# Four token tiles' finishing steps moved from the first half of a loop to the stretch behind it

## The chip, the cores and the metric

One core of one Trainium2 chip runs the whole kernel. The metric is the device time of one execution in microseconds (us), the median over several runs. All tensors between engines live in the core's on-chip memory; matmul results go to PSUM, an accumulation memory from which ScalarE (ACT) or VectorE (DVE) must copy them before the space can be used again. TensorE (PE) multiplies, DVE and ACT do element-wise work, SyncE (SP) issues nearly all DMAs, GpSimd (POOL) does small things. Each engine runs its own instructions in the order in which they were written out; only semaphores join the engines.

## The reference

The input x is 2048 tokens by 1024 channels. The output mixes two branches with a gate for each token:

```python
g = sigmoid((x * gate_w).sum(-1, keepdims=True))
# branch a: 2-D real FFT over (tokens, channels), product with W, back
X = rfft2(x, axes=(-2, -1)) * (w_r + 1j * w_i)
a = irfft2(X, s=(S, D))
# branch b: a diagonal complex recurrence over the tokens
Lam_bar = exp(dt * Lam);  B_bar = ((Lam_bar - 1) / Lam)[:, None] * Bmat
Bu = einsum("bld,pd->blp", x, B_bar)
for t in range(L):
    h = Lam_bar * h + Bu[:, t, :]
y = 2 * einsum("blp,dp->bld", hseq, Cmat).real + x * Dskip
return g * a + (1 - g) * y
```

x and all weights are bf16, and so is the output.

## The kernel before

The FFT branch (generator `gfnet`) is done as dense transforms with small matrices. Its steps are mixed with the first recurrence units and are over at about 200 us; what stays of it is the tile `ZT`, the spectrum after all transforms but the last one along the channels.

The recurrence branch is cut into 8 chunks of 256 tokens and two halves q of the 1024 states, 16 **units** in all. `unit(c, q)` makes 64 matmuls (L209) into two PSUM tiles `psu`, one for the real and one for the imaginary part; ACT copies each into the tile `h` (L211); DVE then rotates, scans (L223) and rotates back (L215 to L234), with a small carry to the next chunk (L227 to L229). A unit of a later chunk must follow the unit of the chunk before.

A chunk holds two **token tiles** of 128 tokens, 16 tiles in all, numbered tb. For each there are two steps:

- `c_gemm(tb)`, the **C product**: 32 matmuls of `h` with `CT` (L462) and 8 of `xT` with a diagonal (L466), into the PSUM tile `ps_y`.
- `finish(tb, psy)`: 8 matmuls (L483) do the last inverse transform of the tile from `ZT` into the PSUM tile `ps_id`; ACT scales it by the gate into a part of the tile `raw` (L486); DVE unfolds it in four operations (L488, L489, L491, L492) into the tile `ga`; DVE adds the C product (L500); SP stores `ga` to the output (L501).

The first four token tiles are **early** (`NEARLY = 4`). Their C products are made while the FFT branch still runs; `early(tb)` stores them as f32 halves in a scratch in DRAM (L475). When `finish` runs for such a tile, it has no `psy`: SP loads each half back into the tile `yl` (L497) and DVE adds it (L498), half by half.

Four buffer rules matter around the change:

- `ps_id` and both `psu` of a unit come from one pool with two PSUM buffers (`psU`). A third use waits until ACT has emptied the first.
- `ps_y` has its own pool of two (`psA`), emptied by DVE's L500.
- The part of `raw` that ACT writes at L486 is chosen by `tb % 2`. Two tiles in a row with the same parity share it: ACT may write the second one only when DVE has read the first (L488, L489).
- `yl` has one buffer, so the second half's load waits for the first half's add, and the next tile's first load for this tile's second add.

The main loop goes over the last 8 units. In it `todo` is the list of tiles 4 to 15, and `late` that of tiles 0 to 3. After the loop four tiles of `todo` are left, 12 to 15. We call the loop's eight passes iterations 0 to 7, and what follows the **tail**. No planner sets the order here: each engine's order is essentially that of the code, with small steps that the framework moves across each other by its priorities.

Of the kernel before, what the change touches and what calls it, by code (L numbers as in the profile page):

```python
# [84 lines left out]
def kernel(  # L85
# [370 lines left out]
    def c_gemm(tb, pool=None, tag="ps"):  # L456
        c, tq = tb // 2, tb % 2
        psy = (pool or psA).tile([P, D], FP32, name="ps_y", tag=tag)
        for dh in range(2):
            for i in range(16):  # L460
                jb, ri = i // 2, i % 2
                nc.tensor.matmul(psy[:, 512 * dh:512 * (dh + 1)], lhsT=hs[c, jb // 4][:, ri, jb % 4, P * tq:P * (tq + 1)],  # L462
                                 rhs=CT[ri][:, jb, 512 * dh:512 * (dh + 1)], start=(i == 0), stop=False)
            for d4 in range(4):
                d8 = 4 * dh + d4
                nc.tensor.matmul(psy[:, P * d8:P * (d8 + 1)], lhsT=xT[:, d8, P * tb:P * (tb + 1)],  # L466
                                 rhs=fft["dgD"][:, d8, :], start=False, stop=(d4 == 3))
        return psy
# [8 lines left out]
    def finish(tb, psy=None):  # L477
        ZT_t = fft["ZT"]
        pse = psU.tile([P, 4, H], FP32, name="ps_id", tag="psu")
        for slot, (cls, ri) in enumerate(((0, 0), (1, 1), (0, 1), (1, 0))):  # L480
            for kb in range(2):
                i = 4 * cls + 2 * kb + ri
                nc.tensor.matmul(pse[:, slot, :], lhsT=ZT_t[:, i, tb, :], rhs=fft["Gi"][:, i, :],  # L483
                                 start=(kb == 0), stop=(kb == 1))
        part = raw[:, D * (2 + tb % 2):D * (3 + tb % 2)].rearrange("p (s c n) -> p s c n", s=2, c=2)
        nc.scalar.activation(out=part.rearrange("p s c n -> p (s c) n"), in_=pse, func=ACT.Copy, scale=gB[:, tb:tb + 1])  # L486
        eo = raw[:, D * (4 + tb % 2):D * (5 + tb % 2)].rearrange("p (c k) -> p c k", c=2)
        nc.vector.tensor_add(out=eo[:, :, 0:H], in0=part[:, 0], in1=part[:, 1])  # L488
        nc.vector.tensor_sub(out=eo[:, :, K - 1:H - 1:-1], in0=part[:, 0], in1=part[:, 1])  # L489
        ga = fft["gq"].tile([P, 2, K], BF16, name="ga")  # L490
        nc.vector.tensor_add(out=ga[:, 0], in0=eo[:, 0], in1=eo[:, 1])  # L491
        nc.vector.tensor_sub(out=ga[:, 1], in0=eo[:, 0], in1=eo[:, 1])  # L492
        o = ga.rearrange("p h n -> p (h n)")
        if psy is None:
            for hf in range(2):
                ye = fft["gq"].tile([P, K], FP32, name="yl", bufs=1)
                nc.sync.dma_start(out=ye, in_=y_dram[tb, hf])  # L497
                nc.vector.tensor_add(out=ga[:, hf], in0=ye, in1=ga[:, hf])  # L498
        else:
            nc.vector.scalar_tensor_tensor(out=o, in0=psy, scalar=omg[:, tb:tb + 1], in1=o, op0=ALU.mult, op1=ALU.add)  # L500
        nc.sync.dma_start(out=out2[P * tb:P * (tb + 1), :], in_=o)  # L501
# [160 lines left out]
    late = list(range(NEARLY))  # L662
    for c in range(4, 8):
        for q in range(2):
            unit(c, q)
            tb = todo.pop(0)
            finish(tb, c_gemm(tb))
            if late:
                finish(late.pop(0))
    for tb in todo:  # L670
        finish(tb, c_gemm(tb))


# [28 lines left out]
```

## Time and profile before

| what | us |
|---|---|
| median of 3 runs (lowest to highest) | 413.42 (412.79 to 415.82) |
| the profiled execution, its own time | 413.43 |
| its span, first to last instruction | 411.6 |
| PE busy | 365.1 (89%) |
| DVE busy | 307.8 (75%) |
| ACT busy | 168.9 (41%) |
| POOL busy | 28.8 (7%) |

The profiled execution takes 1.83 us more than its span, and its time is that of the median. The loop's first matmul starts at 225.49 us of the span, the tail's first at 370.42, and the last output DMA is issued at 408.58. In a row of the timeline stand the start, the duration, the engine, the line, the operation with its output and inputs, the shapes and a count; in square brackets follows how long the engine sat idle before it, and what ended that wait. The word issue there means that the profile shows nothing that was waited for. In a row of the waits stand who waited, for what, and the total, the count and the longest, in us. A view of windows cuts the span into stretches and gives the busy time of each engine with the count of instructions, the granted clock of TensorE (1.00 is full), the DMA share and GB/s.

### The profile page before, as it was taken

What the parts mean: (1) busy time and instruction counts of PE and PEld (TensorE: products, weight loads), DVE (VectorE), ACT (ScalarE), POOL (GpSimd) and SP (SyncE); (2) the same over time, 40 slices, a digit from 0 to 9 for tenths busy, and PEclk for the clock granted to TensorE, in tenths of its full rate; (3) what the DMA queues carried; (4) which work ended last, traced back from release to release, by engine and by line L of the source; (5) the groups of instructions that cost most, each with busy time, mean ns of one, the idle gap of its engine ahead of it and who ended that gap; (6) DMA issues with size and microseconds to landing.
All of it is one profiled execution on the core that took longest, in us unless ns stands there. A gap on an engine that the chain in (4) does not pass through costs nothing. (4 is left out here: it accounts for less than half of the span.)

```text
span 411.6 us, 6481 instructions
## 1 busy us (share of the span) xinstructions
PE 365.1 (89%) x2601; PEld 239.7 (58%) x2601; DVE 307.8 (75%) x477; ACT 168.9 (41%) x210; POOL 28.8 (7%) x68
## 2 busy tenths in 40 slices
PE   4868998999797998999999988689796999999992
PEld 4836555667574454457766765556464767764551
DVE  2873598196989898990098897959696999999332
ACT  2759797664221588848721212121212113202111
POOL 7600011162000000000000000000000000000000
PEclk9879999999899699999999999969898999999997
DMA  7999921987742288659310103011111000000001
GB/s 207 340 201 208 212 77 53 223 191 148 179 146 79 82 274 314 225 173 292 123 53 2 51 2 100 3 51 51 53 51 53 25 27 2 25 27 16 36 32 45
DMA packets 58077, 45.84 MB, mean 111 GB/s; under 512 B 38720, under 2 KB 43200, under 8 KB 57792
## 3 DMA queue, kind: packets, MB, share of 16 engines
q1 hardware_dynamic: 57616, 45.41, 38.8%
q0 software_dynamic: 352, 0.02, 0.7%
q8 instruction: 20, 0.33, 0.3%
q14 instruction: 9, 0.07, 0.1%
q10 hardware_dynamic: 80, 0.01, 0.0%
HBM read 22.35 MB, written 14.69 MB: 90 GB/s over the span
## 5 line engine op out<-in xcount | busy, mean ns | idle before, releaser
L209 PE MATMUL psu<-xT,BT 128*128 128x256 bf16 x1024 | 129.3, 283 | 14.8 <-ACT raw L486 13.4
L209 PEld LDWEIGHTS <-BT 128*128 128x128 bf16 x1024 | 103.1, 101 | 38.8 <-issue 15.8
L462 PE MATMUL ps_y<-CT,h 128*128 128x512 bf16 x512 | 117.2, 379 | 0.7 <-DVE ga L500 0.7
L462 PEld LDWEIGHTS <-h 128*128 128x128 bf16 x512 | 49.5, 98 | 53.2 <-issue 0.9
L223 DVE TENSOR_TENSOR_SCAN h<-rz,h 128x1024 bf16<-128x1024 f32 x32 | 71.8, 2278 | 0.3
L486 ACT ACTIVATE raw<-ps_id,gB 128x1024 bf16<-128x1024 f32 x16 | 17.8, 1113 | 109.1 <-PE ps_id L483 85.5
L215 DVE TENSOR_TENSOR su<-h,tab 128x2048 bf16<-128x2048 bf16 x16 | 19.6, 1222 | 48.6 <-ACT h L211 48.5
L211 ACT CAST h<-psu 128x1024 bf16<-128x1024 f32 x32 | 32.3, 1010 | 57.1 <-PE psu L209 57.1
L249 PE MATMUL ps_fd<-G_sb,preT 128*128 128x512 bf16 x128 | 32.0, 397 | 4.7 <-ACT X L252 4.3
L249 PEld LDWEIGHTS <-preT 128*128 128x128 bf16 x128 | 18.6, 146 | 15.2 <-issue 8.5
L252 ACT CAST X<-ps_fd 128x1024 bf16<-128x1024 f32 x16 | 20.7, 1304 | 9.3 <-PE ps_fd L249 9.3
L359 ACT CAST X<-ps_s 128x1024 bf16<-128x1024 f32 x16 | 16.2, 1013 | 17.1 <-PE ps_s L357 17.1
L216 DVE TENSOR_TENSOR h<-h,tab 128x2048 bf16<-128x2048 bf16 x16 | 19.6, 1222 | 0.5
L488 DVE TENSOR_TENSOR raw<-raw 128x512 bf16<-128x512 bf16 x16 | 6.7, 418 | 17.3 <-ACT raw L486 17.3
L232 DVE TENSOR_TENSOR h<-h,tab 128x2048 bf16<-128x2048 bf16 x16 | 19.6, 1222 | 0.1
L231 DVE TENSOR_TENSOR sg<-h,tab 128x2048 bf16<-128x2048 bf16 x16 | 19.5, 1217 | 0.1
L507 PE MATMUL pt<-ident,BT 128*128 128x128 bf16 x128 | 12.8, 271 | 5.6 <-DMA BT<-in_A_x_dram 5.5
L380 ACT CAST C<-ps_is 128x1024 bf16<-128x1024 f32 x16 | 16.2, 1014 | 3.6 <-PE ps_is L378 3.2
L396 ACT CAST ZT<-ps_is 128x1024 bf16<-128x1024 f32 x16 | 16.1, 1012 | 3.0 <-PE ps_is L394 2.3
L392 PE MATMUL ps_is<-R_sb,raw 128*128 128x256 bf16 x64 | 14.8, 272 | 1.7 <-DMA raw<-turn_scratch 1.7
L500 DVE SCALAR_TENSOR_TENSOR ga<-ps_y,omg,ga 128x1024 bf16<-128x1024 f32 x12 | 15.4, 1283 | 1.2
L483 PE MATMUL ps_id<-raw,ZT 128*128 128x256 bf16 x128 | 15.9, 273 | 0.0
(188 smaller groups left out, 445.9 us busy)
## 6 DMA issues: line engine op xcount, KB each, us to landing
BT<-in_A_x_dram SPq DMA_DIRECT2D x8, 512.0 KB, 6.4
turn_scratch<-A SPq DMA_DIRECT2D x16, 256.0 KB, 2.9
Bb<-turn_scratch SPq DMA_DIRECT2D x16, 256.0 KB, 3.9
turn_scratch<-C SPq DMA_DIRECT2D x16, 256.0 KB, 3.1
raw<-turn_scratch SPq DMA_DIRECT2D x16, 256.0 KB, 5.3
out_dram<-ga SPq DMA_DIRECT2D x16, 256.0 KB, 2.0
W_b<-in_A_w_r_dram SPq DMA_DIRECT2D x16, 128.0 KB, 4.2
W_b<-in_A_w_i_dram SPq DMA_DIRECT2D x16, 128.0 KB, 3.8
```

What stands on the lines that cost most here:

```text
L209: nc.tensor.matmul(psu[:, j, :], lhsT=BT[4 * q + j][:, ri, d8, :], rhs=xT[:, d8, TC * c:TC * (c + 1)], start=(d8 == 0), stop=(d8 == 7))
L211: nc.scalar.copy(out=u[:, ri], in_=psu)
L215: nc.vector.tensor_mul(out=su, in0=u[:, ::-1], in1=bc(1))
L216: nc.vector.tensor_mul(out=u, in0=u, in1=bc(0))
L223: nc.vector.tensor_tensor_scan(out=seg, data0=rz[:, js].rearrange("p j t -> p (j t)"), data1=seg, initial=0.0, op0=ALU.mult, op1=ALU.add)
L231: nc.vector.tensor_mul(out=sg, in0=u[:, ::-1], in1=bc(3))
L232: nc.vector.tensor_mul(out=u, in0=u, in1=bc(2))
L249: nc.tensor.matmul(ps[:, cls, :], lhsT=preT_A[:, cls, d4, j, :], rhs=G_sb[:, cls, d4, :], start=(d4 == 0), stop=(d4 == 3))
L252: nc.scalar.copy(out=X1.rearrange("p r (i c) -> p c r i", c=2), in_=ps.rearrange("p c (r i) -> p c r i", r=2))
L359: nc.scalar.copy(out=X2, in_=ps2)
L462: nc.tensor.matmul(psy[:, 512 * dh:512 * (dh + 1)], lhsT=hs[c, jb // 4][:, ri, jb % 4, P * tq:P * (tq + 1)], rhs=CT[ri][:, jb, 512 * dh:51 ...
L486: nc.scalar.activation(out=part.rearrange("p s c n -> p (s c) n"), in_=pse, func=ACT.Copy, scale=gB[:, tb:tb + 1])
```

## The change

In the loop, `finish` is no longer called for a late tile. In the tail, each C product's `finish` is followed by that of one late tile, so the tail's order is 12, 0, 13, 1, 14, 2, 15, 3. All else is left: the same operations, the same buffers, the same tiles.

```diff
             unit(c, q)
             tb = todo.pop(0)
             finish(tb, c_gemm(tb))
-            if late:
-                finish(late.pop(0))
     for tb in todo:
         finish(tb, c_gemm(tb))
+        finish(late.pop(0))
```

What moves on ACT, in the loop's iterations 0 to 2. `psu` is a unit's PSUM tile, `ps_id` that of a finish. Before:

```order
L486 ACTIVATE raw<-ps_id,gB 128x1024 x2
L211 CAST h<-psu 128x1024 x2
L486 ACTIVATE raw<-ps_id,gB 128x1024 x2
L211 CAST h<-psu 128x1024 x2
L486 ACTIVATE raw<-ps_id,gB 128x1024 x2
```

And the same place now:

```order
L486 ACTIVATE raw<-ps_id,gB 128x1024
L211 CAST h<-psu 128x1024 x2
L486 ACTIVATE raw<-ps_id,gB 128x1024
L211 CAST h<-psu 128x1024 x2
L486 ACTIVATE raw<-ps_id,gB 128x1024
```

The second scaling between two units' copies is gone from iterations 0 to 3, and the row at ACT's end counts 9 in place of 5.

What moves on SP, in the tail. The numbers tell the buffers' uses apart: before, `ga_3911` is tile 11 and `ga_3969` to `ga_4143` are tiles 12 to 15.

```order
L501 DMA out_0_dram<-ga_3911 128x1024
L501 DMA out_0_dram<-ga_3969 128x1024
L501 DMA out_0_dram<-ga_4027 128x1024
L501 DMA out_0_dram<-ga_4085 128x1024
L501 DMA out_0_dram<-ga_4143 128x1024
```

Now `ga_3881`, `ga_3961` and `ga_4041` are tiles 12, 13 and 14, `ga_3898` and `ga_3978` are tiles 0 and 1:

```order
L501 DMA out_0_dram<-ga_3881 128x1024
L497 DMA yl_3904<-y_scratch_60 128x512
L501 DMA out_0_dram<-ga_3898 128x1024
L497 DMA yl_3981<-y_scratch_60 128x512
L501 DMA out_0_dram<-ga_3961 128x1024
L497 DMA yl_3984<-y_scratch_60 128x512
L501 DMA out_0_dram<-ga_3978 128x1024
L497 DMA yl_4061<-y_scratch_60 128x512
L501 DMA out_0_dram<-ga_4041 128x1024
```

Seven of the eight loads of `yl` now stand between the tail's stores; the eighth (tile 0's first half) stands far ahead in both kernels.

What ends DVE's work. Before, tile 15 (`ga_4143`) is the last:

```order
L488 TENSOR_TENSOR raw_512<-raw_512 128x2x256
L489 TENSOR_TENSOR raw_512<-raw_512 128x2x256
L491 TENSOR_TENSOR ga_4143<-raw_512 128x512
L492 TENSOR_TENSOR ga_4143<-raw_512 128x512
L500 SCALAR_TENSOR_TENSOR ga_4143<-ps_y_4090,omg_809,ga_4143 128x1024
```

Now tile 15 is `ga_4121`, and tile 3 (`ga_4138`) is the last:

```order
L500 SCALAR_TENSOR_TENSOR ga_4121<-ps_y_4068,omg_809,ga_4121 128x1024
L488 TENSOR_TENSOR raw_512<-raw_512 128x2x256
L489 TENSOR_TENSOR raw_512<-raw_512 128x2x256
L491 TENSOR_TENSOR ga_4138<-raw_512 128x512
L492 TENSOR_TENSOR ga_4138<-raw_512 128x512
L498 TENSOR_TENSOR ga_4138<-yl_4141,ga_4138 128x512
L498 TENSOR_TENSOR ga_4138<-yl_4144,ga_4138 128x512
```

Behind tile 15's L500 there are now six more DVE operations ahead of the last store, with a load of `yl` between the last two.

## The prediction

> **What bounds the kernel now.** I read the page first, for the engine that works most and the wait that ends its idle time.
>
> ```profile
> span 411.6 us, 6481 instructions
> ...
> L209 PE MATMUL psu<-xT,BT 128*128 128x256 bf16 x1024 | 129.3, 283 | 14.8 <-ACT raw L486 13.4
> ```
>
> The units' matmuls stood idle 14.8 us, 13.4 of them until a scaling of a finish (L486) was over. All of that must lie where finishes run, so I cut the loop and the tail into windows at the starts of the PE work: five rows for iterations 0 to 4, three for 5 to 7, one for the tail.
>
> ```profile
> 225.49:242.07 16.58, 16.58 (x125) 11.60 (x123) 14.58 (x16) 4.40 (x5) 0.00 (x0) 1.00 0.09 33
> 242.07:260.82 18.75, 16.31 (x122) 11.38 (x121) 15.62 (x26) 4.14 (x4) 0.00 (x0) 1.00 0.17 57
> 260.82:284.00 23.18, 18.76 (x122) 12.53 (x121) 18.64 (x27) 4.14 (x4) 0.00 (x0) 0.85 0.14 46
> 284.00:305.25 21.25, 17.97 (x121) 12.28 (x120) 17.51 (x26) 4.14 (x4) 0.00 (x0) 0.92 0.16 50
> 305.25:324.78 19.53, 16.25 (x111) 11.02 (x110) 16.13 (x25) 3.03 (x3) 0.00 (x0) 0.91 0.12 42
> 324.78:340.00 15.22, 15.22 (x115) 10.62 (x113) 14.91 (x20) 3.14 (x3) 0.00 (x0) 1.00 0.05 18
> 340.00:355.21 15.21, 15.21 (x114) 10.62 (x112) 14.90 (x20) 3.14 (x3) 0.00 (x0) 1.00 0.05 18
> 355.21:370.42 15.21, 15.21 (x114) 10.61 (x112) 14.83 (x17) 3.14 (x3) 0.00 (x0) 1.00 0.05 18
> 370.42:404.39 33.97, 33.23 (x194) 17.36 (x191) 17.23 (x26) 4.46 (x4) 0.00 (x0) 1.00 0.08 31
> ```
>
> Here are two regimes of one loop. Iterations 5 to 7, which have one finish each, take 15.21 us with PE busy in all of it and DVE in 14.9. Iterations 0 to 3 have a second, late finish, and with what they leave behind in iteration 4 the five windows take 99.29 us, or 19.9 each. In the tail PE is full again, and DVE is busy in half of it.
>
> The waits from 222 us on say how the late finish does that (waiter, what it waited for, total, count, longest):
>
> ```profile
> ACT raw L486 <- DVE raw L489: 23.6, 4, 7.0
> ...
> PE psu L209 <- ACT raw L486: 13.4, 4, 4.4
> DVE su L215 <- ACT h L211: 12.5, 4, 4.2
> ```
>
> Each has a count of 4, the number of late finishes. The timeline of all engines at iteration 2's end and iteration 3's start shows the links in order:
>
> ```profile
> 280.63 4.48 DVE L223 TENSOR_TENSOR_SCAN h<-rz,h 128x1024 bf16<-128x1024 f32 x2
> ...
> 281.76 1.91 PE L483 MATMUL ps_id<-raw,ZT 128*128 128x256 bf16 x16
> 282.83 1.11 ACT L486 ACTIVATE raw<-ps_id,gB 128x1024 bf16<-128x1024 f32 x1 [6.78 <-PE ps_id L483]
> ...
> 284.00 3.65 PE L209 MATMUL psu<-xT,BT 128*128 128x256 bf16 x32
> ...
> 289.24 0.42 DVE L489 TENSOR_TENSOR raw<-raw 128x512 bf16<-128x512 bf16 x1
> ...
> 289.77 1.11 ACT L486 ACTIVATE raw<-ps_id,gB 128x1024 bf16<-128x1024 f32 x1 [5.82 <-DVE raw L489]
> ...
> 290.93 5.32 PE L209 MATMUL psu<-xT,BT 128*128 128x256 bf16 x32 [3.28 <-ACT raw L486]
> ```
>
> PE makes both finishes' matmuls at once (16 at 281.76). ACT scales the first at 282.83. The second is of a tile with the same parity (6 and 2), so ACT must wait until DVE has read the first; but DVE is in the unit's scans and gets to L489 only at 289.24. Until 290.88 the late `ps_id` holds one of the two `psU` buffers, so PE can make one half of the next unit (284.00) and then stands for 3.28 us. That delays ACT's copies and DVE's next unit (the 12.5 us of the third wait). It is a circle through three engines that only the late finish closes.
>
> **The change, part by part.** The loop first. Its other rows:
>
> ```profile
> 225.49 7.15 PE L209 MATMUL psu<-xT,BT 128*128 128x256 bf16 x64
> ...
> 248.17 3.65 PE L209 MATMUL psu<-xT,BT 128*128 128x256 bf16 x32 [2.44 <-ACT raw L486]
> ...
> 268.89 6.11 PE L209 MATMUL psu<-xT,BT 128*128 128x256 bf16 x32 [4.42 <-ACT raw L486]
> ...
> 312.18 4.97 PE L209 MATMUL psu<-xT,BT 128*128 128x256 bf16 x32 [3.28 <-ACT raw L486]
> ...
> 323.91 1.04 PE L483 MATMUL ps_id<-raw,ZT 128*128 128x256 bf16 x8
> ```
>
> Without the late finishes, iterations 0 to 4 have on each engine the order that 5 to 7 have, so I take their 15.21. The loop's PE work then lasts from 225.49 to 225.49 + 8 x 15.21 = 347.17, where before it ended at 370.42: **23.25 us less**. The parts confirm it. Gone are four times eight L483 matmuls (1.91 - 1.04 = 0.87 each, 3.5 in all); the waits of 2.44, 4.42, 3.28 and 3.28 (13.4); and the slow matmuls behind three of these waits: 32 of them took 6.11, 5.32 and 4.97 where 3.65 is normal (5.4). Together 22.3; the 0.9 left is small gaps. DVE, at 14.8 to 14.9 busy of 15.21, becomes the next limit; it is the cover that has nearly nothing left, and I put 0.7 as the upper bound of what it adds over eight iterations (the 0.72 that PE waits for DVE at the loop's end, row 379.53 below); below zero is excluded, since PE has no idle time to give.
>
> Of the slow matmuls, the trace has full speed behind 2.44 us of idleness, and a lowered clock behind 3.28 and more (0.85 to 0.92 in these windows). [...] The measured rows decide: I count all three as gone.
>
> The tail next. Its PE rows, and the last steps:
>
> ```profile
> 379.53 3.61 PE L462 MATMUL ps_y<-CT,h 128*128 128x512 bf16 x16 [0.72 <-DVE ga L500]
> ...
> 387.76 3.62 PE L462 MATMUL ps_y<-CT,h 128*128 128x512 bf16 x16
> ...
> 395.11 1.04 PE L483 MATMUL ps_id<-raw,ZT 128*128 128x256 bf16 x8
> ...
> 395.99 3.62 PE L462 MATMUL ps_y<-CT,h 128*128 128x512 bf16 x16
> ...
> 403.34 1.04 PE L483 MATMUL ps_id<-raw,ZT 128*128 128x256 bf16 x8
> ...
> 405.61 0.42 DVE L488 TENSOR_TENSOR raw<-raw 128x512 bf16<-128x512 bf16 x1 [5.29 <-ACT raw L486]
> ...
> 407.26 1.28 DVE L500 SCALAR_TENSOR_TENSOR ga<-ps_y,omg,ga 128x1024 bf16<-128x1024 f32 x1
> 408.58 0.33 SPq L501 DMA_DIRECT2D out_dram<-ga  x1
> ```
>
> One C product with its finish takes PE 395.99 - 387.76 = 8.23, 7.35 up to the finish's L483 (395.11). Each late finish adds 0.87. Tile 15's L483 would start at 347.17 + 3 x (8.23 + 0.87) + 7.35 = 381.82, against 403.34: 21.52 earlier. The 0.72 wait on DVE goes by itself: 0.87 of late L483 now stands ahead of that C product.
>
> Then the end. Tile 15's L500 comes 407.26 - 403.34 = 3.92 behind its L483. Behind it follow tile 3's steps, which the loop shows in the same DVE order:
>
> ```profile
> 247.78 1.28 DVE L500 SCALAR_TENSOR_TENSOR ga<-ps_y,omg,ga 128x1024 bf16<-128x1024 f32 x1
> ...
> 251.21 0.32 SPq L497 DMA_DIRECT2D yl<-y_scratch  x1
> ...
> 253.91 0.69 DVE L498 TENSOR_TENSOR ga<-yl,ga 128x512 bf16<-128x512 f32 x1 [2.73 <-DMA yl<-y_scratch]
> ...
> 254.63 0.34 SPq L501 DMA_DIRECT2D out_dram<-ga  x1
> ```
>
> From L500 to the store's issue is 254.63 - 247.78 = 6.85, of which 2.73 is the wait for `yl`'s second load. So the last store is issued at 381.82 + 3.92 + 6.85 = 392.59, against 408.58: **15.99 us earlier**, the tail and the end having given back 7.3 of the 23.25. What follows the last store is left as it was (3.0 to the span's end, 1.83 from there to the execution's time). Against the profiled execution's own 413.43 that makes **397.4 us**; the median of the runs, 413.42, is the same number, so nothing is added.
>
> What is queued behind the new waits: on DVE, behind a late tile's second L498, the next tile's L488. A pair of finishes holds DVE from 2.27 after the L483 (405.61 - 403.34) to 3.92 + 6.82 = 10.74 after it (254.60 - 247.78 is 6.82); the next pair wants DVE at 9.10 + 2.27 = 11.37. So the load has a cover of 0.63 in each pair and costs nothing but at the end. On SP, the loads stand behind stores whose L500 precedes them on DVE anyway, and the next late tile's first load goes out right behind its predecessor's store. On ACT, the parity rule still makes the late L486 wait, now only for L489 of the tile ahead, which DVE comes to at once; and the next L483 that wants its `psU` buffer is a whole C product away.
>
> The landing time of `yl` is the one price with little behind it. The nearest rows, from the page's DMA issues (name, count, KB, median us to landing):
>
> ```profile
> raw<-turn_scratch SPq DMA_DIRECT2D x16, 256.0 KB, 5.3
> out_dram<-ga SPq DMA_DIRECT2D x16, 256.0 KB, 2.0
> ```
>
> At 2.0 the end is 0.7 earlier, at 5.3 it is 2.6 later. I keep 2.73: it is the same transfer, and the 5.3 were measured with sixteen loads in a row, while the tail's DMA share is 0.08.
>
> **The rivals.**
>
> The loads pace the tail. If each `yl` load takes the 5.3 of the other scratch, a pair needs 8.47 + 2.6 = 11.07 on DVE against PE's 9.10; the lag grows by 1.97 over three pairs, and the end is 3 x 1.97 + 2.6 = 8.5 later: 405.9. For it speaks that DVE's cover is only 0.63, and that stores and loads now share one queue within 9 us; against it the 2.73 measured behind an output store, as in the tail. Still faster. Chance 0.12.
>
> The circle stays closed by something else. If the second finish were not what holds PE, the loop would lose only its 4 x 0.87, and the tail and the end would cost their full price: -3.5 + 2.6 (three L483 groups) - 0.7 + (10.77 - 5.24) = +3.9, so 417.4, slower by 0.95%. Against it speaks that iterations 5 to 7 run the new order with no wait. Chance 0.03, half of it beyond 1%.
>
> The clock does not hold: the change makes PE dense from 225 to 382, 156 us without a gap. If the clock is lowered under such a load, PE paces everything: 156.3/f - 156.3 more, at the lowest mean of these windows (0.85) 27.6, so 425.0. It turns to slower by 1% (20.1 more) where f is under 0.886. For it: 0.85 to 0.92 in three windows. Against it: these are the windows with waits, while 1.00 is granted from 324.78 to 404.39, 79.6 us with PE idle for 0.7. [...] Chance 0.03.
>
> **How the numbers follow.** The forecast, 397.4, has 0.82. Its own range is 0.7 down for the landing and 0.6 for the lowest of the runs (412.79), and up 0.7 for DVE, 2.6 for a late last load and some of the 2.4 by which the highest run lay above the median. So the range is 395.5 to 401.5, and its upper end takes in the milder half of the loads' rival. About 1% is what a measurement of this kernel can tell from no change. Faster by more than that: the forecast and the loads' rival, 0.94. Within 1%: 0.02. Slower by over 1%: the clock and half of the other rival, rounded up for a wait not thought of, 0.04.
>
> **What would show it.** In the changed profile, the L209 group's idle time should fall from 14.8 to about 1, with no wait on L486; all eight iterations should be 15.2 apart with the clock at 1.00; `ACT raw <- DVE raw` should fall from 23.6 to a few us; tail C products should start 9.1 apart with no PE wait; the chain at the end should show one wait of 2 to 3 us for `yl` between two L498. The prediction is wrong if iterations 0 to 3 still exceed 16, if DVE waits for `yl` grow along the tail, or if the clock falls without an idle stretch before it.

## The result, and the profile after

| | median us (lowest to highest) | ratio to the kernel before, 95% interval |
|---|---|---|
| before | 414.13 (412.79 to 415.82) | |
| changed | 396.36 (395.47 to 398.15) | 0.9574 (0.9523 to 0.9625) |

The change takes 4.3% off; 397.4 was forecast. The profiled execution after takes 396.32, with a span of 394.5. The page of the changed kernel, and its loop and tail cut at the starts of the PE work as before (stretch, then its length, busy us of PE, weight loads, DVE, ACT and POOL, the granted clock, DMA share, GB/s); shown are iterations 0, 1 and 7, the tail's PE work, and all of it in one row:

```profile
span 394.5 us, 6484 instructions
...
L209 PE MATMUL psu<-xT,BT 128*128 128x256 bf16 x1024 | 122.9, 275 | 1.2 <-DMA BT<-in_B_B_re_dram 1.2
```

```profile
224.35:239.56 15.21, 15.21 (x115) 10.63 (x113) 13.22 (x16) 3.29 (x4) 0.00 (x0) 1.00 0.10 36
239.56:254.78 15.22, 15.22 (x115) 10.62 (x112) 14.91 (x20) 3.14 (x3) 0.00 (x0) 1.00 0.05 18
...
330.84:346.06 15.22, 15.22 (x115) 10.63 (x113) 14.84 (x17) 3.14 (x3) 0.00 (x0) 1.00 0.05 17
346.06:382.46 36.40, 36.40 (x226) 20.49 (x223) 24.60 (x43) 8.48 (x8) 0.00 (x0) 1.00 0.24 80
224.35:382.46 158.11, 158.11 (x1123) 105.47 (x1120) 142.02 (x188) 33.74 (x33) 0.00 (x0) 1.00 0.10 34
```

The units' matmuls no longer wait for a scaling at all; their 1.2 us of idleness is a weight's DMA at the start. From the loop's first matmul to the last one of the kernel PE is busy for all of 158.11 us, with the clock at 1.00. The waits from 222 us on (waiter, what for, total, count, longest):

```profile
DVE ga L498 <- DMA yl<-y_scratch: 11.0, 4, 2.8
...
ACT raw L486 <- DVE raw L489: 3.6, 4, 0.9
DVE raw L488 <- ACT raw L486: 3.3, 4, 1.4
DVE su L215 <- ACT h L211: 1.7, 1, 1.7
```

The late scaling still waits for DVE four times, but 0.9 us each, where it was up to 7.0. DVE now waits for a load four times (11.0 us in total), where the kernel before shows one such wait of 2.7. The timeline of the tail (start, duration, engine, line, operation, idle time ahead of it and its releaser) shows where both lie:

```profile
353.41 1.91 PE L483 MATMUL ps_id<-raw,ZT 128*128 128x256 bf16 x16
...
355.16 3.62 PE L462 MATMUL ps_y<-CT,h 128*128 128x512 bf16 x16
...
356.56 1.12 ACT L486 ACTIVATE raw<-ps_id,gB 128x1024 bf16<-128x1024 f32 x1 [0.91 <-DVE raw L489]
...
363.42 0.69 DVE L498 TENSOR_TENSOR ga<-yl,ga 128x512 bf16<-128x512 f32 x1 [2.73 <-DMA yl<-y_scratch]
...
364.26 3.62 PE L462 MATMUL ps_y<-CT,h 128*128 128x512 bf16 x16
...
380.71 1.91 PE L483 MATMUL ps_id<-raw,ZT 128*128 128x256 bf16 x16
...
384.59 1.28 DVE L500 SCALAR_TENSOR_TENSOR ga<-ps_y,omg,ga 128x1024 bf16<-128x1024 f32 x1
...
387.97 0.33 SPq L497 DMA_DIRECT2D yl<-y_scratch  x1
390.76 0.69 DVE L498 TENSOR_TENSOR ga<-yl,ga 128x512 bf16<-128x512 f32 x1 [2.82 <-DMA yl<-y_scratch]
391.48 0.33 SPq L501 DMA_DIRECT2D out_dram<-ga  x1
```

PE goes from pair to pair in 9.10 (355.16 to 364.26) without seeing either wait. Only the last pair's load stands on the path, between 387.97 and 390.76.

In the experiments I use one more measure: from the loop's first matmul to the issue of the last store, read from the profiles. It leaves out what lies ahead of the loop, where all of these kernels have the same code but for tile 0's first load. It is 408.58 - 225.49 = 183.09 before and 391.48 - 224.35 = 167.13 after, so 15.96 less.

### The profile page after: what moved, and what is told of

Same layout as the page of the kernel before. It is cut to its first block, busy times and chain, and to the rows that moved or that the text cites. A ratio compares the mean times of both kernels' runs of the same rounds, so it can differ in the third digit from the quotient of the medians.

```text
span 394.5 us, 6484 instructions
## 1 busy us (share of the span) xinstructions
PE 356.9 (90%) x2601; PEld 236.9 (60%) x2601; DVE 308.3 (78%) x477; ACT 168.6 (43%) x210; POOL 28.6 (7%) x68
## 4 chain that ended last, share of the span: by engine, by line
PE 70%; DMA 11%; ACT 7%; DVE 6%; issue 2%; SPq 1%; POOLq 1%; POOL 0%; ACTq 0%; DVEq 0%
PE ps_y L462 26%; PE psu L209 22%; PE ps_fd L249 6%; PE ps_id L483 3%; ACT X L252 3%; DMA BT<-in_A_x_dram 3%; DMA Bb<-turn_scratch 2%; DMA W_b<-in_A_w_r_dram 2%; PE ps_is L392 2%; PE ps_y L466 2%; PE ps_is L394 2%; DMA raw<-turn_scratch 1%; DVE h L223 1%; DMA vec<-in_B_log_dt_dram 1%; DMA BT<-in_B_B_re_dram 1%
## 5 line engine op out<-in xcount | busy, mean ns | idle before, releaser
L209 PE MATMUL psu<-xT,BT 128*128 128x256 bf16 x1024 | 122.9, 275 | 1.2 <-DMA BT<-in_B_B_re_dram 1.2
L209 PEld LDWEIGHTS <-BT 128*128 128x128 bf16 x1024 | 100.7, 99 | 20.4 <-DMA BT<-in_B_B_re_dram 1.5
L486 ACT ACTIVATE raw<-ps_id,gB 128x1024 bf16<-128x1024 f32 x16 | 17.8, 1115 | 86.6 <-PE ps_id L483 83.0
L249 PE MATMUL ps_fd<-G_sb,preT 128*128 128x512 bf16 x128 | 31.0, 387 | 4.7 <-ACT X L252 4.3
L359 ACT CAST X<-ps_s 128x1024 bf16<-128x1024 f32 x16 | 16.2, 1013 | 16.8 <-PE ps_s L357 16.8
L380 ACT CAST C<-ps_is 128x1024 bf16<-128x1024 f32 x16 | 16.2, 1014 | 3.8 <-PE ps_is L378 3.4
L500 DVE SCALAR_TENSOR_TENSOR ga<-ps_y,omg,ga 128x1024 bf16<-128x1024 f32 x12 | 15.4, 1283 | 1.2
L483 PE MATMUL ps_id<-raw,ZT 128*128 128x256 bf16 x128 | 15.9, 273 | 0.0
L267 POOL COPY Acol<-A 128x2 bf16<-128x2 bf16 x16 | 9.9, 617 | 68.4 <-DVE A L266 35.4
```

What stands on the lines that cost most here:

```text
L209: nc.tensor.matmul(psu[:, j, :], lhsT=BT[4 * q + j][:, ri, d8, :], rhs=xT[:, d8, TC * c:TC * (c + 1)], start=(d8 == 0), stop=(d8 == 7))
L249: nc.tensor.matmul(ps[:, cls, :], lhsT=preT_A[:, cls, d4, j, :], rhs=G_sb[:, cls, d4, :], start=(d4 == 0), stop=(d4 == 3))
```

## The experiments

Two explanations stood against each other. The circle: a late finish in the loop shares the part of `raw` with the tile ahead, so ACT waits for DVE, `ps_id` holds a `psU` buffer, PE stands, and DVE's next unit is late. DVE's extra work: four late finishes put some 2.7 us of DVE work each (1.5 from L488 to L498, twice 0.6 for the adds), and their load waits, into iterations in which DVE already works 14.9 of 15.2. Both go with the change, so its result can't tell them apart.

### The circle opened at the parity

```diff
-    late = list(range(NEARLY))
+    late = [1, 0, 3, 2]
```

> The kernel before with the late tiles in the order 1, 0, 3, 2, so that a late tile in the loop never has the parity of the tile ahead of it; same work, same places. Circle theory (the late scaling waits for DVE, holds a psU buffer, and PE stands): the 13.4 us in which PE waits for L486 fall to under 1, the granted clock in the loop is 1.00, and what stays is DVE's extra work, 4 x 2.7 us and one or two waits of 2.7 for loads: the stretch from the loop's first matmul to the tail's is 135 to 138 us (144.9 before, 121.7 after), the time 404 to 407. Rival, DVE's extra work alone makes the loop long: that work is all still there, so the stretch stays at 145 and the time at 413 to 414.

Measured: 409.71, a ratio of 0.9933 (0.9903 to 0.9962), neither of the two. The waits, a window over the whole loop, DVE from one unit's scan to the next, and the tail's PE:

```profile
PE ps_y L462 <- DVE ga L500: 11.4, 2, 6.5
...
DVE ga L498 <- DMA yl<-y_scratch: 8.5, 4, 2.7
```

```profile
225.86:351.43 125.57, 125.57 (x931) 88.06 (x929) 113.78 (x155) 29.27 (x29) 0.00 (x0) 1.00 0.12 41
```

```profile
238.23 4.48 DVE L223 TENSOR_TENSOR_SCAN h<-rz,h 128x1024 bf16<-128x1024 f32 x2
...
253.73 0.69 DVE L498 TENSOR_TENSOR ga<-yl,ga 128x512 bf16<-128x512 f32 x1 [2.67 <-DMA yl<-y_scratch]
...
258.41 4.47 DVE L223 TENSOR_TENSOR_SCAN h<-rz,h 128x1024 bf16<-128x1024 f32 x2
```

```profile
358.15 5.49 PE L462 MATMUL ps_y<-CT,h 128*128 128x512 bf16 x16 [6.55 <-DVE ga L500]
...
363.70 3.62 PE L462 MATMUL ps_y<-CT,h 128*128 128x512 bf16 x16
...
373.31 6.43 PE L462 MATMUL ps_y<-CT,h 128*128 128x512 bf16 x16 [4.90 <-DVE ga L500]
```

The circle is open: no wait of PE for L486 is left, and PE runs through the loop in 125.57 us, 19.4 less than before (144.93). (In this order it is the regular tile behind a late one that shares its part of `raw`. ACT waits for that once, 8.7 us, and PE does not.) But DVE could not follow. While PE's iterations take 16.2, DVE's scans follow each other in 20.2, 20.0, 19.0 and 19.1 (238.23, 258.41, 278.39, 297.41, 316.55): 17.3 of work, and a load wait of 1.6 to 2.7 that the circle had covered in three of four iterations. In the kernel before they came 20.7 to 22.0 apart, so DVE alone is nearly as slow as the circle.

DVE carries its late work on as a debt of which PE learns only in the tail, where two C products wait 6.55 and 4.90 us for tile 10's and tile 11's L500 to free `ps_y`. Behind each wait the granted clock is low (a mean of 0.75 from 351.43 to 365.00 and of 0.66 from 373.00 to 382.00, and 1.00 from there to 400.00) and the next 16 matmuls take 5.49 and 6.43 in place of 3.62. From the tail's start to tile 15's L483 it takes 48.50 (399.93 - 351.43) in place of 32.92 (403.34 - 370.42): 15.6 of the 19.4 are given back. My range of 404 to 407 had the debt too small: I had counted one or two load waits of 2.7 where four came to 8.5, and nothing for the slow matmuls, which cost 4.7 (1.87 and 2.81).

### The circle kept, DVE's late work taken out

```diff
-                finish(late.pop(0))
+                finish_bare(late.pop(0))
```

The new `finish_bare` (not shown) makes the tile's eight matmuls and its scaling, and stores the scaled part.

> The kernel before, where a late tile in the loop has only its eight matmuls and its scaling (same parity as before); its DVE steps and its loads are left out and the scaled part itself is stored, so the first 512 tokens' output is not the mix. Circle theory: the late scaling still waits for L489, PE still waits for it, 2 to 4 us four times, and only the DVE work that lay on the circle goes (1.6 in iteration 0, 0.6 in the others): stretch 141 to 142, time 410. Rival, DVE's extra work: DVE is back at 14.9 per iteration and PE at 16.1, so the stretch is 125, the time 394.

Measured: 410.88, a ratio of 0.9945 (0.9906 to 0.9983). The waits, one iteration's window, and the link in the timeline (L513 is the late scaling here):

```profile
DVE su L215 <- ACT h L211: 23.6, 5, 5.5
ACT raw L513 <- DVE raw L489: 21.0, 4, 5.3
...
PE psu L209 <- ACT raw L513: 10.9, 4, 2.8
```

```profile
261.12:281.90 20.78, 17.97 (x121) 12.27 (x120) 14.97 (x20) 4.14 (x4) 0.00 (x0) 0.92 0.07 26
```

```profile
286.67 0.42 DVE L489 TENSOR_TENSOR raw<-raw 128x512 bf16<-128x512 bf16 x1
...
287.20 1.11 ACT L513 ACTIVATE raw<-ps_id,gB 128x1024 bf16<-128x1024 f32 x1 [5.35 <-DVE raw L489]
...
288.36 5.32 PE L209 MATMUL psu<-xT,BT 128*128 128x256 bf16 x32 [2.81 <-ACT raw L513]
...
294.76 1.23 DVE L215 TENSOR_TENSOR su<-h,tab 128x2048 bf16<-128x2048 bf16 x1 [5.50 <-ACT h L211]
```

The circle theory's 410 is met, and the rival's 394 is not. DVE has 15.0 us of work in an iteration of 20.78 and waits for the rest of it; the circle alone holds the loop nearly as long as before: 143.55 us from its first matmul to the tail's (367.68 - 224.13) in place of 144.93. That is more than the 141 to 142 expected; behind the first of the four waits 32 matmuls took 1.7 more than in the kernel before (last section).

### Both taken out

```diff
-    late = list(range(NEARLY))
+    late = [1, 0, 3, 2]
...
-                finish(late.pop(0))
+                finish_bare(late.pop(0))
```

> Both edits that were tried singly, together: the kernel before with the late tiles in the order 1, 0, 3, 2 (no parity wait) and with a late tile's DVE steps and loads left out (the first 512 tokens' output is then not the mix). Two-bounds theory (the circle, and DVE's work with its load waits, each hold the loop by themselves, so that taking one away shows the other): now the loop is held by neither, PE paces it at 15.21 with 0.9 more in four iterations, 125 us from the loop's first matmul to the tail's, no wait of PE on L500 in the tail, and the time is 394 +- 1.5. Rival, the gains of the single edits add up (3.9 and 2.7): 407.

Measured: 392.61, a ratio of 0.9513 (0.9466 to 0.956), as the two-bounds theory has it. The loop and the tail:

```profile
223.45:349.02 125.57, 124.61 (x919) 88.11 (x929) 117.35 (x146) 29.27 (x29) 0.00 (x0) 1.00 0.08 28
349.02:382.50 33.48, 33.02 (x190) 17.33 (x191) 16.75 (x25) 4.46 (x4) 0.00 (x0) 1.00 0.09 32
```

The loop is as short as with the parity alone, and nothing is given back in the tail. In the measure from the loop's first matmul to the last store:

| | circle closed | circle open |
|---|---|---|
| DVE's late work in the loop, with its loads | 183.09 | 179.31 |
| without it | 181.25 | 163.25 |

Either cause alone keeps the stretch nearly as long as both. Taking one away is worth 3.8 or 1.8 us, taking both 19.8. Each cell is one profile; the medians, each against the kernel before on its own chip, say the same: 3.9, 2.7 and 20.0. The change takes both, since in the tail DVE has room for the work and no unit waits behind it.

### The circle opened at the other link

```diff
-        pse = psU.tile([P, 4, H], FP32, name="ps_id", tag="psu")
+        pse = (psA if psy is None else psU).tile([P, 4, H], FP32, name="ps_id",
+                                                 tag="ps" if psy is None else "psu")
```

> The kernel before, where a late tile's ps_id takes a buffer of the C products' pool instead of one of the units' pool; the parity stays, so the late scaling still waits for DVE. Circle theory with the held psU buffer as its link: PE makes both halves of the next unit at once and no longer waits for L486; DVE's work paces the loop at 17.6: stretch 135 to 138, time 404 to 407. If it is enough that ACT stands (its copies of the next unit queue behind the late scaling): stretch about 145, time 413. DVE's extra work alone: 413 too.

Measured: 405.18, a ratio of 0.9822 (0.9763 to 0.988). The waits and the loop's window:

```profile
ACT raw L486 <- DVE raw L489: 28.8, 4, 8.7
...
PE ps_y L462 <- ACT raw L486: 7.2, 3, 3.1
...
PE ps_y L462 <- DVE ga L500: 3.6, 1, 3.6
```

```profile
224.51:359.00 134.49, 127.34 (x931) 88.53 (x929) 124.30 (x167) 28.87 (x29) 0.00 (x0) 0.99 0.12 40
```

ACT's wait for DVE is longer than before (28.8 against 23.6 in total), yet the units' matmuls wait for nothing: the held `psU` buffer is the link that stops them, and ACT's standing alone is not. The C products wait instead. The 7.2 us are the same hold in a milder place: the late `ps_id` now keeps a buffer of `ps_y` until its scaling. The 3.6 are DVE's debt. Time and stretch are near what was expected (134.49 against 135 to 138), but not by a DVE that paces the loop at 17.6: its scans come 19.3 apart (256.16, 275.52, 294.86), PE's first two iterations still take 16.1, and the tail pays for part of it. From the loop's first matmul to the last store it is 177.22 (401.73 - 224.51), 5.9 less than before: more than with the parity alone, and still far from 19.8.

### Late tiles first in the tail

```diff
     for tb in todo:
-        finish(tb, c_gemm(tb))
         finish(late.pop(0))
+        finish(tb, c_gemm(tb))
```

> The changed kernel, where each late tile in the tail is finished ahead of the C product instead of behind its finish, so that tile 15 is the last. By the sum of the prediction: PE's tail is as long as in the changed kernel plus 0.9 (tile 15's L483 at 35.5 behind the tail's start instead of 34.65), but the end is 5.24 behind it instead of 10.77: 4.7 less, about 391.7, a ratio of 0.946 to the kernel before. Rival, the late tile's loads and DVE steps now delay the tile behind them on DVE (the cover is 0.6 a pair): up to 2 to 4 us of it is lost, 394 to 396.

Measured: 391.85, a ratio of 0.9502 (0.944 to 0.9565). Tile 15's L483, its L500, and the last two stores' row (start of the first, time to the end of the last):

```profile
380.20 1.04 PE L483 MATMUL ps_id<-raw,ZT 128*128 128x256 bf16 x8
...
382.56 3.21 SPq L501 DMA_DIRECT2D out_dram<-ga  x2
...
384.13 1.28 DVE L500 SCALAR_TENSOR_TENSOR ga<-ps_y,omg,ga 128x1024 bf16<-128x1024 f32 x1
```

The last store is issued at 382.56 + 3.21 - 0.33 = 385.44, 5.24 behind tile 15's L483, and 162.47 behind the loop's first matmul (222.97): 4.66 less than in the changed kernel, as the sum had it. Once more beside the changed kernel on one chip:

> Late tiles first in the tail, once more, beside the changed kernel on the same chip: 4.7 less than it, 391.7 +- 1, a ratio of 0.946. If the difference of the first run was one of chips, both come out alike.

> The changed kernel once more, beside late-first on the same chip: 396.4 +- 1, a ratio of 0.957 to the kernel before.

Measured: 392.66, a ratio of 0.9511 (0.9472 to 0.9549), and for the changed kernel 395.91, a ratio of 0.9574 (0.9541 to 0.9607). By the profiles 162.56 and 167.01. The intervals overlap slightly, since the runs of one kernel spread by 3 to 5 us; the measure inside the profile repeats within 0.12 and is 4.45 lower here. This version beats both kernels.

### The loads ahead

```diff
-                ye = fft["gq"].tile([P, K], FP32, name="yl", bufs=1)
+                at = 4 * (tb % 2) + 2 * hf
+                ye = rz[:, at:at + 2, :].rearrange("p j t -> p (j t)")
```

With that in the changed kernel:

> The changed kernel, where the late tiles' halves are loaded into the scan's table rz, which is free after the last unit, so that four halves fit instead of one and the second half is loaded ahead. By the prediction's sum the load's wait costs only at the end, 2.7 to 2.8 us once, though the profile shows it four times (11.0 in total): 393.6, a ratio of 0.950 to the kernel before if the changed kernel has 0.9574. If each of the four waits cost, 385.

Measured: 394.23, a ratio of 0.9546 (0.951 to 0.9582). The end, with L499 and L502 for the adds and stores:

```profile
387.17 2.99 SPq L502 DMA_DIRECT2D out_dram<-ga  x2
...
388.52 1.28 DVE L499 TENSOR_TENSOR ga<-rz,ga 128x512 bf16<-128x512 f32 x2
```

All four load waits are gone, and from the loop's first matmul (225.62) to the last store (387.17 + 2.99 - 0.33 = 389.83) it takes 164.21: 2.9 less, the price of one wait, not of four. And with late tiles first:

> Late tiles first in the tail, and their halves loaded ahead into rz. With tile 15 last, no load wait is left on the path that ends the kernel; the four waits go, and nothing is gained: 391.7 +- 1, as with late tiles first alone (391.85). Rival, DVE's cover of 0.6 a pair was not enough: 2 to 3 us less, 389.

Measured: 391.67, a ratio of 0.9501 (0.946 to 0.9543), and 162.47 by the profile (386.27 - 223.80), the same as without the loads ahead. The cover of 0.6 us a pair is small, but it is enough; a wait under it costs nothing.

### The parity in the tail

```diff
-    late = list(range(NEARLY))
+    late = [1, 0, 3, 2]
```

> The changed kernel with the late tiles in the order 1, 0, 3, 2, so that in the tail no late scaling waits for DVE (four waits of 0.9, 3.6 in total). The next matmul that wants the PSUM buffer is a C product away, so nothing is gained: 396.4 +- 1, where the same edit in the loop of the kernel before took PE's waits away. If these waits cost, 393.

Measured: 397.45, a ratio of 0.9638 (0.9591 to 0.9686), 1.5 us above the changed kernel's second median (on another chip), which by itself would read as slightly worse. The profile puts it elsewhere: the loop's first matmul comes at 226.49 there against 224.78, and from it to the last store (393.45) it takes 166.96, against 167.13 and 167.01. The four waits of 0.9 are gone, and nothing is gained: the wait that closed the circle in the loop is harmless in the tail.

## Why the prediction was right, and where it was not

- **The loop.** 8 x 15.21 = 121.68 was forecast from the loop's first matmul to the tail's; it is 346.06 - 224.35 = 121.71. DVE, for which I had put up to 0.7, added nothing.
- **The tail.** Pairs of 9.10 and tile 15's L483 at 34.65 behind the tail's start: 9.10, and 380.71 - 346.06 = 34.65. PE's wait of 0.72 went by itself, as said.
- **The end.** 10.77 from that L483 to the last store: 391.48 - 380.71 = 10.77. The load's wait, the price with the least behind it, was 2.82 where 2.73 was taken. It did not grow along the tail (2.73, 2.77, 2.69, 2.82), so the loads' rival fell.
- **The 1.1 us left over.** The changed kernel's loop starts 1.14 earlier (224.35 against 225.49), in code that is the same. In the twelve profiles here that start lies between 222.97 and 226.49, so I take it for chance; the sum itself forecast 15.99 less, and 15.96 was measured.
- **The clock.** It was 1.00 through 158.11 dense us (224.35 to 382.46), so that rival fell too; its chance of 0.03 was my estimate. The slow matmuls behind the waits went with the waits, as I had counted them: a unit's 64 matmuls take 7.15 us in all eight iterations.
- **What I had wrong** is the step that took the gain apart: "It is a circle through three engines that only the late finish closes", and the list of 13.4 us of waits and 5.4 of slow matmuls beside it. The circle is there, and opening either link frees the units' matmuls. But the list reads as if ending those waits were worth their sum, and with the circle open 15.6 of 19.4 us came back in the tail. I had seen that DVE's cover "has nearly nothing left", and priced it for the loop without the late work only; I did not ask what DVE would have done with the late work and without the waits, which is to need 19.0 to 20.2 us for what PE does in 16.2: 17.3 of work and a load wait. So the circle was not the only thing that made the loop long; DVE was a second bound of nearly the same length. The number was right all the same because it was taken from iterations 5 to 7, which lack both causes, and not from the sum of the waits.
- **The rival of a circle that stays closed** had its half of the truth there: something else does hold the loop, but it goes with the same change.

## What to carry to other kernels

The time that an engine waits for another is not what ending the wait is worth: ask what the engine that was waited for would then have to do, and whether there is room for it. Where two causes each hold a stage by themselves, taking away one shows next to nothing, and the four cases of a two-by-two tell it. A stage that runs the wanted order already, like iterations 5 to 7 here, priced this move within 0.03 us in the loop; and what is moved to the end should not be the last thing there.

## What the runs showed of the hardware that was not expected

The clock falls behind shorter waits than the prediction's rows suggested. In the run without DVE's late work, PE waited 2.45 us ahead of one unit's second half and 2.81 ahead of three others, and all four took 5.27 to 5.32 in place of 3.65, at a mean granted clock of 0.91 to 0.92 in the iterations that hold them:

```profile
246.81 5.32 PE L209 MATMUL psu<-xT,BT 128*128 128x256 bf16 x32 [2.45 <-ACT raw L513]
...
267.58 5.32 PE L209 MATMUL psu<-xT,BT 128*128 128x256 bf16 x32 [2.81 <-ACT raw L513]
```

In the kernel before, a wait of 2.44 cost nothing: its 32 matmuls took 3.65 at a granted clock of 1.00. And in the run with the late `ps_id` in the C products' pool, a wait of 2.62 cost nothing either, while one of 3.11 cost 1.7 us:

```profile
266.46 3.61 PE L462 MATMUL ps_y<-CT,h 128*128 128x512 bf16 x16 [2.62 <-ACT raw L486]
...
285.82 5.30 PE L462 MATMUL ps_y<-CT,h 128*128 128x512 bf16 x16 [3.11 <-ACT raw L486]
```

So the wait's length alone does not decide between 2.4 and 2.7 us: 2.45 was slow, 2.62 was not. What else decides is not shown by these runs.

And part of the spread of the runs lies ahead of the loop: its first matmul moves by up to 3.5 us between the profiles, while from there to the last store the two kernels that were profiled twice repeat within 0.12 us. What moves it was not tried, and of the kernels in which the units' matmuls wait there is one profile each.
